# Exponential blocks for VectorE taken also from the next head segment, their products added one part at a time, and a normalisation with three buffers and its broadcast on another queue

## The chip, the cores and the metric

One core of a Trainium2 chip. The metric is device time in microseconds (us) from start to end of one execution. Every kernel was run once with a profile and, except for the first look at the kernel before, three times more, always next to runs of the kernel before on the same chip.

Names: PE is TensorE (matrix products, written to the banks of the memory PSUM), ACT is ScalarE (the exponentials), DVE is VectorE, POOL is GpSimd and SP is SyncE; the last two issue transfers (DMA) here. The engines run side by side, each through its own list of instructions.

## The reference, cut to what matters

Two transformer layers on 2048 tokens of width 512: attention with 32 heads of size 16, then a dense layer of width 1792 with ReLU, each behind a layer norm and with a residual.

```python
qkv = (x @ wqkv).reshape(B, S, 3, H, Dh).transpose(2, 0, 3, 1, 4)     # H = 32, Dh = 16
scores = jnp.einsum("bhqd,bhkd->bhqk", q, k) * (Dh ** -0.5)
p = softmax(scores, axis=-1)
o = jnp.einsum("bhqk,bhkd->bhqd", p, v)
...
x = x + A(layernorm(x)); x = x + B(layernorm(x))                      # this pair twice
```

What costs the time is the softmax's exponential: 2 layers x 32 heads x 2048 x 2048 scores.

## The kernel before

The scores are made in blocks of 128 keys x 512 queries, 4,096 of them. Three blocks make a **slot**: nine (or three, or more) score matmuls write three PSUM banks, one exponential on ScalarE turns them into bf16, and some slots later three product matmuls add them to `ps_o`. A **segment** is the work of four heads for one chunk of 512 queries: 16 key blocks x 4 heads = 64 blocks, 21 slots and a third. A head has only 16 dimensions, so a score matmul uses 32 of the 128 rows of the array, and `g`, the head's place in the group of four, says which 32.

In some slots ScalarE gets only two of the three blocks. VectorE makes the third exponential with integer and polynomial steps; it does so for two slots together, a **pair**. All instructions are put in order by a planner in the kernel's own Python, which keeps estimated clocks (`now_pe`, `now_dve`, `exp_end`) and decides from them. Other matrix products (projections, dense layer) are *owed* in pieces and fitted in between; when five or more are owed, a piece may go ahead past its time limit. That is the *hurry* of the change and of x11; *pace* is how many pieces a slot must take.

The planner's lists of VectorE's work, and a pair's chain of five steps and its six product matmuls:

```python
            if not can:
                for t in dve_q:
                    ready = at(t["deps"], "dve")
                    if ready is not None:
                        can.append((2, ready, t))          # pair chains and everything else alike
...
        steps = (
            (690, lambda: bits(dm, 0x007FFFFF, 0x3E800000)),
            (1260, lambda: step(dy, dm, C2, dm)),
            (1260, lambda: step(dy, dy, C1, dm)),
            (1260, lambda: step(de, dy, C0, di)),
            (690, lambda: bits(di, 0x7F800000, KAPPA_BITS)),
        )
        for n, (cost, fn) in enumerate(steps):
            k = key + (n,) if n + 1 < len(steps) else key
            task(cost, fn, [k], [key + (n - 1,)] if n else [], place=sum("chain" in t for t in dve_q))

    def emit_pair():
        p = pairs.popleft()
        pe_run("v", 3, at([p["key"]], "pe"))
        halves = list(enumerate(p["blocks"]))
        tops = p["di"][:].bitcast(BF16)
        for rhs in (de, de, None):
            for half, (kb, g) in halves:
                pv(p["sg"], kb, g, tops[:, half, 1::2] if rhs is None else rhs[:, half, :])
```

The end of a segment (normalisation): the sums are copied out of `ps_o`, four rows of them go to `c`, VectorE takes the reciprocal, and they come back and are broadcast to `r`, which multiplies `u`:

```python
        if n > 1:
            run_until(("m", n - 2))                         # two buffers
        u, r, c = ubuf[n % 2], rbuf[n % 2], cbuf[n % 2]
...
        def copy():
            nc.vector.tensor_copy(out=u[:], in_=ps_o[:])    # or tensor_add with stored sums
            mark(("po",))
            if not last:
                nc.sync.dma_start(out=c[:], in_=sums)       # 8 KB
                mark(("c", n), lag=2600.0)
...
        def recip():
            nc.vector.reciprocal(out=c[:], in_=c[:])
            nc.sync.dma_start(out=sums, in_=c[:])
            nc.sync.dma_start(out=r[:], in_=...)            # 256 KB, each row of sums to 32 partitions
            mark(("r", n), lag=8500.0)
```

The slot, with the choice of pairs after the scores:

```python
        spare = int(max(need_by - pe_start("s", s_ready), 0.0) / MM)
        short = FLOOR * 1330.0 - level - busy[0] - MM * (1 + (len(pend) > 1))
        times = 1 + min(spare, max(0, math.ceil(short / MM)))    # repeats keep PE busy
        for _ in range(times):
            for w, (sg, kb, g) in enumerate(now):
                nc.tensor.matmul(b[:, w, :], kt[32 * g : 32 * g + 32, kc : kc + P], ...,
                                 tile_position=(32 * g, 0))
        half = None
        if len(now) == W and now[0][0] is sg and not sg["busy"]:
            r = (kb * 4 + g - 2) // W
            if pair_at is not None:
                half = 1 if r == pair_at + 2 else None
            elif len(pairs) < 2 and ...:
                if (
                    ends < now_pe[0] + (21 - r) * 1280.0 + LATE      # in time for this segment's end
                    and now_dve[0] + waiting < now_pe[0] + BACKLOG
                ):
                    half = 0
```

A pair must be complete before its segment's sums can be copied, so no pair is begun near a segment's end.

The softmax here doesn't subtract the row's maximum and nothing guards it: scores larger than these inputs give would overflow.

## Time and profile before

| | before |
|---|---|
| device time, median | 1831.78 us (1831.12 to 1832.17) |
| profiled run, span | 1828.2 us |
| ScalarE busy | 1751.7 us, 96% |
| VectorE busy | 1172.0 us, 64% |
| exponentials of 1536 / 1024 / 512 columns | 1,129 / 236 / 1 |
| first exponential begins, last ends | 17.0 us, 1777.5 us |

A bound of this kind is best read by a budget: the time the exponentials would take if each followed the last at its usual step, and what is lost beside it. The first part of the page holds the busy shares and the chain of work that ended last. The second part shows, in 40 equal slices of the span, VectorE's busy tenths and the granted clock of PE:

```profile
DVE  7436767777676876778442323586678668667673
...
PEclk9999999999999999999999996999999999999998
```

VectorE has room nearly everywhere, and the clock has a dent in the 25th slice. The windows (columns: length, then busy time with number of instructions for PE, PE's weight loads, VectorE, ScalarE, GpSimd, then granted clock, DMA share, GB/s) give the first layer, the stretch of the dent, and the 3.4 us before the clock fell:

```profile
102.00:850.00 748.00, 700.24 (x5803) 220.54 (x5869) 539.94 (x777) 747.02 (x594) 31.47 (x42) 1.00 0.09 19
1085.00:1152.00 67.00, 59.21 (x436) 14.74 (x437) 25.41 (x38) 52.87 (x40) 0.00 (x0) 0.72 0.13 26
1109.60:1113.00 3.40, 0.72 (x10) 0.32 (x12) 2.62 (x5) 0.86 (x1) 0.00 (x0) 1.00 0.05 7
```

In the second row ScalarE works 52.87 of 67 us; elsewhere it hardly rests.

### The profile page before, as it was taken

What the parts mean: (1) busy time and instruction counts of PE and PEld (TensorE: products, weight loads), DVE (VectorE), ACT (ScalarE), POOL (GpSimd) and SP (SyncE); (2) the same over time, 40 slices, a digit from 0 to 9 for tenths busy, and PEclk for the clock granted to TensorE, in tenths of its full rate; (3) what the DMA queues carried; (4) which work ended last, traced back from release to release, by engine and by line L of the source; (5) the groups of instructions that cost most, each with busy time, mean ns of one, the idle gap of its engine ahead of it and who ended that gap; (6) DMA issues with size and microseconds to landing.
All of it is one profiled execution on the core that took longest, in us unless ns stands there. A gap on an engine that the chain in (4) does not pass through costs nothing.

```text
span 1828.2 us, 31187 instructions
## 1 busy us (share of the span) xinstructions
PE 1684.4 (92%) x13531; PEld 533.0 (29%) x13706; DVE 1172.0 (64%) x1795; ACT 1751.7 (96%) x1388; POOL 86.4 (5%) x147
## 2 busy tenths in 40 slices
PE   8899999999999999999999888999999999999987
PEld 3223332222232222322222332232222322232223
DVE  7436767777676876778442323586678668667673
ACT  7999999999999999999999997999999999999981
POOL 1000000100001000010010000001000110001001
PEclk9999999999999999999999996999999999999998
DMA  4000000110001000010000001001000110001101
GB/s 144 1 13 8 19 14 10 39 25 12 8 19 47 8 13 10 23 41 13 13 24 18 1 16 29 13 16 43 16 21 11 34 35 14 16 13 36 28 22 41
DMA packets 38989, 42.37 MB, mean 23 GB/s; under 512 B 19268, under 2 KB 27204, under 8 KB 38852
## 3 DMA queue, kind: packets, MB, share of 16 engines
q1 hardware_dynamic: 32132, 24.37, 5.9%
q0 software_dynamic: 5376, 14.69, 2.9%
q8 instruction: 107, 1.75, 0.4%
q10 hardware_dynamic: 1344, 1.31, 0.2%
q14 instruction: 30, 0.25, 0.0%
HBM read 20.71 MB, written 2.10 MB: 12 GB/s over the span
## 4 chain that ended last, share of the span: by engine, by line
ACT 82%; PE 11%; DVE 4%; DMA 2%; issue 1%; DVEq 0%; SPq 0%
ACT e L957 82%; PE ps_s L934 4%; PE ps_o L722 3%; PE ps_f L378 3%; PE ps_s L1012 1%; DMA c<-u 1%; DVE dy L793 1%; DVE di L763 1%; DVE de L793 0%; DMA r<-u 0%; DVE dm L787 0%; DVE vaug L516 0%; DVE stats L397 0%; PE ps_f L1012 0%; DVE ktp L488 0%
## 5 line engine op out<-in xcount | busy, mean ns | idle before, releaser
L957 ACT ACTIVATE e<-ps_s 128x1536 bf16<-128x1536 f32 (+1 forms) x1366 | 1738.8, 1517 | 22.1 <-PE ps_s L934 21.3
L934 PE MATMUL ps_s<-q,ktp 32*128 32x512 bf16 x7284 | 777.1, 384 | 99.7 <-ACT e L957 77.8
L722 PE MATMUL ps_o<-e,vaug 128*32 128x512 bf16 x3860 | 546.8, 393 | 6.0 <-DVE u L668 4.5
L934 PEld LDWEIGHTS <-ktp 32*128 32x128 bf16 x7284 | 232.2, 92 | 531.3 <-issue 460.3
L722 PEld LDWEIGHTS <-vaug 128*32 128x32 bf16 x4568 | 162.7, 93 | 493.6 <-issue 467.2
L763 DVE TENSOR_SCALAR di<-ps_s 128x512 int32<-128x512 f32 x236 | 162.1, 688 | 91.9 <-PE ps_s L934 89.4
L556 POOL DMA_DIRECT2D w<-in_B_w_dram x112 | 84.0, 750 | 1729.1 <-PE ps_f L378 1594.1
L793 DVE SCALAR_TENSOR_TENSOR de<-dy,di 128x1024 bf16<-128x1024 f32 x118 | 144.3, 1223 | 9.4 <-PE ps_o L722 2.4
L793 DVE SCALAR_TENSOR_TENSOR dy<-dm 128x1024 f32<-128x1024 f32 x118 | 144.1, 1221 | 2.5
L793 DVE SCALAR_TENSOR_TENSOR dy<-dy,dm 128x1024 f32<-128x1024 f32 x118 | 144.0, 1221 | 2.1
L566 DVE TENSOR_SCALAR ht<-ps_f 128x512 bf16<-128x512 f32 x98 | 67.5, 689 | 107.2 <-PE ps_f L378 101.6
L378 PE MATMUL ps_f<-xn2T,w 128*128 128x512 bf16 x346 | 114.3, 384 | 5.9 <-issue 1.9
L378 PE MATMUL ps_f<-w,ht 128*128 128x512 bf16 x349 | 110.6, 384 | 4.1 <-issue 3.0
L681 DVE SCALAR_TENSOR_TENSOR ot<-u,mask,r 128x512 bf16<-128x512 f32 (+1 forms) x67 | 46.5, 694 | 71.1 <-DMA r<-u 70.9
L787 DVE TENSOR_SCALAR di<-di 128x1024 int32<-128x1024 int32 x118 | 82.0, 695 | 3.2
L525 DVE TENSOR_SCALAR q<-ps_f,qmask 128x512 bf16<-128x512 f32 x78 | 55.7, 745 | 42.9 <-PE ps_f L378 41.0
L722 PE MATMUL ps_o<-de,vaug 128*32 128x512 bf16 x472 | 82.9, 382 | 0.0
L787 DVE TENSOR_SCALAR dm<-di 128x1024 int32<-128x1024 int32 x118 | 81.5, 691 | 1.5
L378 PE MATMUL ps_f<-xnT,wqkv 128*128 128x512 bf16 x235 | 77.5, 386 | 4.6 <-issue 2.1
L378 PE MATMUL ps_f<-wo,ot 128*128 128x512 bf16 x195 | 63.9, 384 | 2.9 <-issue 2.2
L722 PE MATMUL ps_o<-di,vaug 128*32 128x512 bf16 x236 | 57.7, 391 | 0.0
L670 DVE COPY u<-ps_o 128x512 f32<-128x512 f32 x48 | 33.1, 690 | 29.5 <-PE ps_o L722 29.3
(89 smaller groups left out, 536.2 us busy)
## 6 DMA issues: line engine op xcount, KB each, us to landing
r<-u SPq DMA_DIRECT2D x63, 256.0 KB
w<-in_B_w_dram POOLq DMA_DIRECT2D x112, 128.0 KB, 2.6
out_dram<-x SPq DMA_DIRECT2D x16, 128.0 KB
x<-in_A_x_dram SPq DMA_DIRECT2D x14, 128.0 KB
w<-in_B_w_dram SPq DMA_DIRECT2D x1, 1792.0 KB
wqkv<-in_A_wqkv_dram ACTq DMA_DIRECT2D x2, 512.0 KB
c<-u SPq DMA_DIRECT2D x63, 8.0 KB
u<-c SPq DMA_DIRECT2D x63, 8.0 KB
```

What stands on the lines that cost most here:

```text
L378: nc.tensor.matmul(b, lhsT, rhs, start=(i == 0), stop=(i == n - 1))
L525: return nc.vector.tensor_scalar(out=qbuf[n % 2][e][:], in0=b, scalar1=qmask[e][:, 0:1], scalar2=None, op0=ALU.mult)
L556: nc.gpsimd.dma_start(out=w1buf[n % NW1][:], in_=B_w1[:, ft * P : (ft + 1) * P].rearrange("(c p) f -> p c f", p=P),)
L566: nc.vector.tensor_scalar(out=ht[ft], in0=b, scalar1=0.0, scalar2=None, op0=ALU.max)
L670: nc.vector.tensor_copy(out=u[:], in_=ps_o[:])
L681: nc.vector.scalar_tensor_tensor(out=ot[t][:, a : a + w], in0=u[:, a : a + w], scalar=mask[e][:, 0:1], in1=r[:, a : a + w], op0=ALU.mult, ...
L722: nc.tensor.matmul(ps_o[32 * g : 32 * g + 32, :], vaug[sg["l"]][kb][:, 4 * sg["T"] + g, 2 * e : 2 * e + 32], rhs, start=g not in sg["begun ...
L763: first = nc.vector.tensor_scalar(out=di[:, half, :].bitcast(I32), in0=src, scalar1=EXP_BIAS, scalar2=0.0, op0=ALU.add, op1=ALU.max,)
L787: nc.vector.tensor_scalar(out=out[:].bitcast(I32), in0=di[:].bitcast(I32), scalar1=keep, scalar2=put, op0=ALU.bitwise_and, op1=ALU.bitwise_or,
L793: nc.vector.scalar_tensor_tensor(out=out[:], in0=x[:], scalar=c, in1=y[:], op0=ALU.add, op1=ALU.mult)
L934: nc.tensor.matmul(b[:, w, :], kt[32 * g : 32 * g + 32, kc : kc + P], qbuf[sg["n"] % 2][sg["e"]][32 * g : 32 * g + 32, :], start=True, sto ...
L957: ex = nc.scalar.activation(out=eb[:, :m, :], in_=b[:, :m, :], func=ACTF.Exp, scale=1.0 / (LOG2E * UNIT),)
```

## The change

The intent: more of the exponentials on VectorE, since ScalarE is the bound. Where a pair of the present segment would come too late, its two blocks may come from the next segment, whose end is far off. For that to be affordable, the pair chains get the lowest priority on VectorE; the pair's products are added a part (two matmuls) at a time where PE has room; the normalisation gets three buffers and its large broadcast another queue. Cut to its core:

```diff
+    NU = 3
...
+    HURRY = 2.0
...
-    acc = [x[:, k, :] for x in [dm, dy] + dis for k in range(2)]
+    acc = [... for x in kt01 + kt2] + [... for x in va2]     # layer 1's stored sums: in dead K and V tiles of layer 0
...
-    de = sb([P, 2, QS], BF16, "de")
+    des = [sb([P, 2, QS], BF16, f"de{n}") for n in range(2)]
...
-            limit_now = limit if owed[0] < 5.0 else now_pe[0] + 1000.0
+            limit_now = limit if owed[0] < 5.0 or not hurry[0] else now_pe[0] + 1000.0
...
-                        can.append((2, ready, t))
+                        can.append((3 if "chain" in t else 2, ready, t))
...
-        if n > 1:
-            run_until(("m", n - 2))
-        u, r, c = ubuf[n % 2], rbuf[n % 2], cbuf[n % 2]
+        if n >= NU:
+            run_until(("m", n - NU))
+        u, r, c = ubuf[n % NU], rbuf[n % NU], cbuf[n % NU]
...
-            nc.sync.dma_start(
+            nc.gpsimd.dma_start(
                 out=r[:],
...
-            task(cost, fn, [k], [key + (n - 1,)] if n else [], place=sum("chain" in t for t in dve_q))
+            task(cost, fn, [k], [key + (n - 1,)] if n else [])
...
-    def emit_pair():
-        p = pairs.popleft()
-        pe_run("v", 3, at([p["key"]], "pe"))
+    def emit_pair(limit):
+        p = pairs[0]
+        ready = at([p["key"]], "pe")
+        while p["parts"] and pe_start("v", ready) + MM <= limit:
+            rhs = p["parts"].pop(0)
+            pe_run("v", 1, ready)
+            for half, (kb, g) in enumerate(p["blocks"]):
+                pv(p["sg"], kb, g, rhs(half))
...
+            later = next((x for x in itertools.islice(blocks, 70) if x[0] is not mine), None)
+            if pair_at == no:
+                half, take = 1, pairs[-1]["sg"]
+            elif len(pairs) < 2 and ...:
+                if now_dve[0] + waiting < now_pe[0] + BACKLOG:
+                    if not mine["busy"] and ends < now_pe[0] + left_here * 430.0 - 1300.0:
+                        half, take = 0, mine
+                    elif (
+                        left_here < 40 and later and not later[0]["busy"]
+                        and later[0]["l"] == mine["l"] and not pairs_for(later[0])
+                        and at([("q", later[0]["n"])], "pe") is not None
+                    ):
+                        half, take = 0, later[0]
+            if half is not None:
+                pair_at = no + 2 if half == 0 else None
+                if take is not mine:
+                    blocks.appendleft(now.pop())
+                    now.append(later)
+                    blocks.remove(later)
...
-            emit_pair()
+            emit_pair(max(exp_end[no - 1] + ACT_TO_PE, exp_end[no] - MM - PE_TO_ACT - SWITCH - 100.0))
```

## The prediction

> **What bounds the kernel now.** I read the busy line and the chain of work that ended last, then the groups kept apart by shape, then ScalarE's waits, then the timeline where it waits.
>
> ```profile
> PE 1684.4 (92%) x13531; PEld 533.0 (29%) x13706; DVE 1172.0 (64%) x1795; ACT 1751.7 (96%) x1388; POOL 86.4 (5%) x147
> ...
> ACT 82%; PE 11%; DVE 4%; DMA 2%; issue 1%; DVEq 0%; SPq 0%
> ```
>
> ScalarE (ACT) is busy 96% and makes 82% of the chain: 1,366 exponentials, one per "slot" of three 128x512 score blocks. PE's 92% is no bound: 7,284 score matmuls are issued for 4,096 score blocks, the other 3,188 are repeats that keep it busy.
>
> ```profile
> L957 ACT ACTIVATE e<-ps_s 128x1536 bf16<-128x1536 f32 x1129 | 1557.4, 1594 | 19.9 <-PE ps_s L934 19.1
> L957 ACT ACTIVATE e<-ps_s 128x1024 bf16<-128x1024 f32 x236 | 259.7, 1150 | 2.3 <-PE ps_s L934 2.2
> L763 DVE TENSOR_SCALAR di<-ps_s 128x512 int32<-128x512 f32 x236 | 162.1, 688 | 91.9 <-PE ps_s L934 89.4
> L793 DVE SCALAR_TENSOR_TENSOR de<-dy,di 128x1024 bf16<-128x1024 f32 x118 | 144.3, 1223 | 9.4 <-PE ps_o L722 2.4
> L787 DVE TENSOR_SCALAR di<-di 128x1024 int32<-128x1024 int32 x118 | 82.0, 695 | 3.2
> ```
>
> In 236 slots VectorE takes the third block (118 pairs), so ScalarE does 1024 columns instead of 1536. Successive instructions overlap, so their means cannot be subtracted. I took start-to-start times from the trace: median 1.331 us after a 1536-column exponential, 0.904 us after a 1024-column one. **A block moved to VectorE saves 0.427 us.**
>
> With these steps the ideal run of the exponentials is 1129 x 1.331 + 236 x 0.904 + 0.5 = 1716.5 us. The trace's run is from 16.99 to 1777.5 = 1760.5 us, so 44 us are lost between. By place: about 7.5 us in the first 102 us, 17.4 us between 1093 and 1152 us, and 19 us thinly spread over all the rest. Before the first and after the last exponential stand 17.0 and 50.7 us. The median device time, 1831.8, is 3.6 us over the profiled span, 1828.2.
>
> The 17.4 us are one event. First the chain in order of time, then the SP queue's issues, the timeline of PE and ACT, and the windows:
>
> ```profile
> 1085.78 0.70 DVE u L668
> 1086.47 0.02 issue
> 1086.49 5.01 DMA c<-u
> ...
> 1103.16 6.30 DMA c<-u
> ```
>
> ```profile
> 1102.58 0.53 SPq L691 DMA_DIRECT2D r<-u  x1
> 1103.16 0.52 SPq L673 DMA_DIRECT2D c<-u  x1
> ```
>
> ```profile
> 1112.28 0.40 PE L722 MATMUL ps_o<-e,vaug 128*32 128x512 bf16 x4 [3.62 <-DVE u L668]
> ...
> 1113.76 1.45 ACT L957 ACTIVATE e<-ps_s 128x1536 bf16<-128x1536 f32 x1 [3.30 <-PE ps_s L934]
> ...
> 1115.71 1.45 ACT L957 ACTIVATE e<-ps_s 128x1536 bf16<-128x1536 f32 x1 [0.49 <-PE ps_s L934]
> ```
>
> ```profile
> 1114.00:1130.00 16.00, 15.53 (x97) 3.18 (x95) 2.95 (x6) 11.97 (x9) 0.00 (x0) 0.50 0.15 30
> 1130.00:1150.00 20.00, 19.53 (x109) 3.65 (x109) 13.28 (x16) 13.65 (x11) 0.00 (x0) 0.50 0.07 15
> ```
>
> This is the second half of layer 1's first chunk, where a head segment has only 16 blocks and lasts 16/3 x 1.331 = 7.1 us. Each ends in a normalisation: sums to c, reciprocal, back to u, broadcast to r. The 8 KB transfer c<-u is issued behind the 256 KB r<-u of the segment before, on the same SP queue, and takes 5 to 6.3 us. So these loops run at 9.0 us (1094.19, 1103.16, 1112.25), slower than segments arrive. With two u/r/c buffers the lag ends in a wait: ps_o isn't emptied, PE stands 3.62 us, its granted clock falls to 0.50 for some 36 us (seventh number of the last two rows), and every exponential there waits 0.5 us for scores.
>
> **What the Trainium skill says.** "ScalarE: Activation LUTs", What ACT_TABLE_LOAD costs: 0.833 ns a column; the trace agrees, 0.427 us for 512 columns. "VectorE: DVE Perf Modes", the perf-mode tier table: fp32 scalar operations on SBUF run at twice the rate of two-input ones; the trace agrees, 695 against 1223 ns. "TensorE: Matmul & The Clock Gate", Part 1: a window of about 3.4 us of idleness halves PE's clock. The trace agrees on the fall (3.62 us idle, clock 0.50), but shows a return only after about 36 us, not after one busy window. "DMA: Bandwidth & Descriptors", SWDGE vs HWDGE vs iDMA: the engines take turns between the queues of the two kinds, and SWDGE descriptors need an SBUF path that VectorE can lock. The trace has no r<-u on the GpSimd queue, so neither is shown yet.
>
> **The change part by part.**
>
> *More pairs.* The built programs, read in order: 1,129 / 236 / 1 exponentials of 1536 / 1024 / 512 columns become 1,067 / 298 / 1. That is 149 pairs instead of 118, of which 53 take their blocks from the next segment. 62 blocks x 0.427 = **26.5 us off ScalarE**. None are added in the first chunk of layer 1: its first half stays excluded because it stores sums, its second because its runs are short.
>
> *Cost on VectorE.* A pair is 2 x 0.688 + 2 x 0.693 + 3 x 1.222 = 6.43 us; 31 x 6.43 = 199 us. From 102 to 850 us it is busy 540 of 748 us; 16 pairs more, in 14 us less, make 643 of 734, 88%. The second layer's stretch gives the same. It fits, as the added priority lets other tasks pass the chains, but there is less slack. The first step now ends a median 0.57 us after its slot's exponential begins (99th percentile 1.2), ahead of when its bank is wanted.
>
> *PE.* 124 more product matmuls net, 588 fewer score matmuls: no bound. But a borrowed block comes with its own row group of the array, and in 84 of the 106 borrowed slots it is the row group of one of the two others, so these matmuls cannot overlap; the planner doesn't count that. 15 of the 84 issue the scores three times, 23 twice, 46 once. By an estimate from the 216 ns the kernel's plan gives a pass, and about 0.87 us between a bank's release and the need for its scores, that costs 0.45 us in 15 slots, 0.1 in 23 and 0.05 in 46: **+11 us at worst, I take 7**.
>
> *One part at a time, and no hurry below a pace of 2.* Six product matmuls at once delay scores; in the trace the slots around them lose 4.9 us in all, and single delays of 0.3 us elsewhere some 3 us. I take **-5 us**. More 1024-column slots, each losing 0.044 us on average, **+3**, and a fuller VectorE **+3**. So the thin losses go from 19 to 27.
>
> *Three buffers, r on the GpSimd queue.* c no longer stands behind r. A segment's normalisation has 3 x 7.1 = 21 us against an estimated 13 to 14 us (kernel's lags 3.0 and 9.5 us plus VectorE), so PE should not stop and its clock should not fall: **17.4 becomes about 2, -15.4 us**.
>
> *The start* is the same instruction for instruction for the first 300 score matmuls, so its loss of about 7 us stays.
>
> *The tail.* Before, the last-but-one normalisation gets its reciprocal only at 1771.9, behind pair chains, and VectorE waits 2.07 us for r<-u before the last normalisation, which begins at 1781.4. In the new order the reciprocal comes one and a half chains before the end: **about -2.5 us**.
>
> Sum: 17.0 + (1067 x 1.331 + 298 x 0.904 + 0.5 = 1690.1) + 7 + 2 + 27 + 48.2 + 3.6 = 1794.9. Against 1831.8 that is 36.9 us less, 2.0%. I have been cautious with the 7 us for row groups, and the wait constants have plainly been fitted to measurements, so I go a little below: **1792 us**.
>
> **The rivals.**
> (a) *The spared time comes back as waits of ScalarE for scores*: a VectorE at 88%, in fixed order, empties banks and sums late, or row groups collide more dearly. For: the 89.4 us it now waits for scores before its first steps is most of its slack. Against: its steps run at or below the planned durations (1.22 us against 1.26). With 0.1 us lost in each of 298 slots and all row-group costs: about 1810.
> (b) *The new r<-u is slow*: GpSimd is locked out by the VectorE steps of the fast mode (298 of 0.69 us), or stands in its queue behind a weight load waiting for PE; then a VectorE that waits for r in order stops everything. Against: the weight loads on that queue land in a median 2.6 us. For: untested here. If the stall at 1093 to 1152 stays whole: about 1808.
> (c) *It was only the stall*: if nearly all thin loss goes too, 1780.
>
> **Range and chances.** The exponentials' 26.5 us are nearly sure, the stall's 15 likely. What remains open is the thin loss, 15 to 40 us, and that alone moves the time by 25. 8 in 10: 1780 to 1806. The 2% line lies at 1795.1, hardly above my sum: faster 0.57, same 0.42, slower 0.01.
>
> **What would show it.** Right: 1,067 and 298 exponentials with steps of 1.331 and 0.904 us; no wait of ScalarE over 1 us after 110 us; no stretch of granted clock near 0.5 in the middle; c<-u landing in about 2 to 3 us; VectorE near 1,370 us busy. The row-group step is wrong if slots with a borrowed block lose no more than other 1024-column slots. The prediction falls if the clock still drops near the layer's first chunk, or if ScalarE's summed waits for scores exceed some 40 us.

## The result, and the profile after

| | before | after |
|---|---|---|
| device time, median of 4 runs | 1831.65 us (1831.12 to 1832.17) | 1798.97 us (1797.80 to 1800.75) |
| ratio | | 0.9822 (95% interval 0.9805 to 0.9839) |
| profiled run, span | 1828.2 us | 1795.7 us |

The ratio is the mean time of one kernel's runs over that of the other's of the same rounds, so not quite the ratio of the medians; so it is for every ratio below. At a threshold of 2%: "same", 1.8% less.

The busy line, the 40 slices and the chain on the page of the kernel after:

```profile
PE 1657.4 (92%) x13064; PEld 515.0 (29%) x13242; DVE 1356.0 (76%) x2012; ACT 1729.2 (96%) x1388; POOL 133.8 (7%) x210
...
DVE  7438688889989898888642315999888898898863
...
PEclk9999999999999999999999999999999999999999
...
ACT 77%; PE 19%; DVE 2%; issue 1%; DMA 1%; DVEq 0%; ACTq 0%
...
r<-u POOLq DMA_DIRECT2D x63, 256.0 KB, 7.1
```

The dent in the clock is gone and VectorE is fuller by 184 us. But PE's share of the chain has gone *up*, from 11% to 19%: ScalarE waits for PE in more places, each of them short. The last line is the broadcast on its new queue, 7.1 us from issue to landing: in 45 of the 46 times when no other transfer shared the queue, the trace has at most four of its packets under way at once. The groups by shape confirm the new numbers of exponentials:

```profile
L1009 ACT ACTIVATE e<-ps_s 128x1536 bf16<-128x1536 f32 x1067 | 1485.5, 1562 | 9.1 <-PE ps_s L1002 7.8
L1009 ACT ACTIVATE e<-ps_s 128x1024 bf16<-128x1024 f32 x298 | 324.4, 1089 | 6.3 <-PE ps_s L1002 5.2
```

And the windows, first the same 748 us, then the stretch in which the kernel before stood still:

```profile
102.00:850.00 748.00, 699.86 (x5604) 211.22 (x5672) 634.32 (x891) 743.29 (x600) 54.20 (x72) 1.00 0.09 20
1075.00:1130.00 55.00, 49.29 (x461) 16.50 (x464) 32.69 (x48) 54.52 (x43) 4.79 (x7) 1.00 0.20 36
```

ScalarE now works 54.52 of 55 us there. In the first layer VectorE is at 634 of 748 us, 85%.

The full budget, from the start times of the 1,366 exponentials in both traces. A slot's loss is its start-to-start time over the usual step, the most frequent one (1.331 us after 1536 columns, 0.904 us after 1024; both traces give these; the median after 1024 columns, which holds waits too, is 0.912 before and 0.905 after). Slots 672 to 865 are the first chunk of layer 1 and what follows it, where the stall was:

| us | before | after | predicted |
|---|---|---|---|
| until the first exponential | 17.0 | 16.9 | 17.0 |
| exponentials at their steps | 1716.5 | 1690.1 | 1690.1 |
| lost in slots 1 to 75 | 7.9 | 6.6 | 7 |
| lost in slots 75 to 672 | 10.5 | 17.4 | |
| lost in slots 672 to 865 | 19.0 | 3.1 | |
| lost after slot 865 | 6.3 | 13.8 | |
| (the last three together) | 35.8 | 34.3 | 29 |
| after the last exponential | 50.7 | 47.6 | 48.2 |

So of the 32.5 us by which the span shrank, 26.4 are the exponentials handed over and 3.1 the tail. The stall's end gave about 16 more, and nearly all of it went back into slots that start a little late. This is where the expected gain went, and the experiments ask why.

The chain in order of time shows how such a loss looks. First the kernel after, around a segment's end:

```profile
140.29 0.98 PE ps_o L748 x9
...
142.15 1.47 PE ps_s L1002 x9
143.62 0.02 issue
143.64 17.21 ACT e L1009 x14
160.85 0.04 issue
160.89 0.82 PE ps_s L1002 x9
...
169.53 1.41 PE ps_s L1002 x9
170.95 0.02 issue
170.97 2.37 ACT e L1009 x2
```

Nine score matmuls are three passes over three blocks. At 160.89 they take 0.82 us, at 142.15 and 169.53 1.4 to 1.5 us. The slow ones belong to slots in which a borrowed block has the same `g`, the same 32 rows of the array, as another block of the slot: 87 slots of the built program. The Trainium skill, "TensorE: Matmul & The Clock Gate", Part 3 (The mechanism), says that a weight load overlaps running matmuls only when its row group differs; this trace agrees, with 0.6 us more for nine matmuls. By the start times these 87 slots lose 14.9 us: 47 with one pass 0.074 each, 24 with two passes 0.187, 16 with three passes 0.433. (The expectation of x1 counted 13.9 us.)

The tail, in VectorE's timeline, before and after:

```profile
1771.91 0.24 DVE L689 RECIPROCAL c<-c 128x16 f32<-128x16 f32 x1
...
1780.74 0.75 DVE L681 SCALAR_TENSOR_TENSOR ot<-u,mask,r 128x512 bf16<-128x512 f32 x1 [2.07 <-DMA r<-u]
...
1781.41 0.72 DVE L702 STREAM_SHUFFLE r<-u 128x512 f32<-128x512 f32 x1
```

```profile
1728.09 0.24 DVE L715 RECIPROCAL c<-c 128x16 f32<-128x16 f32 x1
...
1748.62 0.69 DVE L695 COPY u<-ps_o 128x512 f32<-128x512 f32 x1 [7.93 <-PE ps_o L748]
...
1749.36 0.72 DVE L728 STREAM_SHUFFLE r<-u 128x512 f32<-128x512 f32 x1
```

Before, the last normalisation (the shuffle) began 3.9 us after the last exponential's end (1777.5), behind a wait for the normalisation ahead of it. After, it begins 1.2 us behind that end (1748.2), with nothing of the earlier normalisation in its way: that one's reciprocal came 20.1 us ahead of the last exponential's end, and not 5.6.

### The profile page after: what moved, and what is told of

Its sections match the earlier page's. It is cut to its first block, busy times and chain, and to the rows that moved or that the text cites. A ratio compares the mean times of both kernels' runs of the same rounds, so it can differ in the third digit from the quotient of the medians.

```text
span 1795.7 us, 30592 instructions
## 1 busy us (share of the span) xinstructions
PE 1657.4 (92%) x13064; PEld 515.0 (29%) x13242; DVE 1356.0 (76%) x2012; ACT 1729.2 (96%) x1388; POOL 133.8 (7%) x210
## 4 chain that ended last, share of the span: by engine, by line
ACT 77%; PE 19%; DVE 2%; issue 1%; DMA 1%; DVEq 0%; ACTq 0%
ACT e L1009 77%; PE ps_s L1002 7%; PE ps_o L748 5%; PE ps_f L397 4%; PE ps_s L1065 1%; DMA wqkv<-in_A_wqkv_dram 1%; DVE di L794 1%; PE ps_f L1065 0%; DVE vaug L535 0%; DVE u L695 0%; DVE stats L416 0%; DVE ktp L507 0%; DVE q L544 0%; PE ps_o L1065 0%; DMA x<-in_A_x_dram 0%
## 5 line engine op out<-in xcount | busy, mean ns | idle before, releaser
L1009 ACT ACTIVATE e<-ps_s 128x1536 bf16<-128x1536 f32 (+1 forms) x1366 | 1716.3, 1459 | 15.3 <-PE ps_s L1002 13.0
L1002 PE MATMUL ps_s<-q,ktp 32*128 32x512 bf16 x6696 | 753.5, 379 | 83.7 <-ACT e L1009 63.4
L794 DVE TENSOR_SCALAR di<-ps_s 128x512 int32<-128x512 f32 x298 | 204.8, 687 | 106.3 <-PE ps_s L1002 104.0
L825 DVE SCALAR_TENSOR_TENSOR dy<-dm 128x1024 f32<-128x1024 f32 x149 | 182.1, 1222 | 4.4
L825 DVE SCALAR_TENSOR_TENSOR dy<-dy,dm 128x1024 f32<-128x1024 f32 x149 | 181.5, 1218 | 3.3
L825 DVE SCALAR_TENSOR_TENSOR de<-dy,di 128x1024 bf16<-128x1024 f32 x149 | 180.6, 1212 | 1.8
L717 POOL DMA_DIRECT2D r<-u x63 | 45.6, 723 | 1245.2 <-DMA u<-c 472.6
L748 PE MATMUL ps_o<-de,vaug 128*32 128x512 bf16 x596 | 110.1, 382 | 0.0
L819 DVE TENSOR_SCALAR dm<-di 128x1024 int32<-128x1024 int32 x149 | 105.4, 708 | 0.6
L819 DVE TENSOR_SCALAR di<-di 128x1024 int32<-128x1024 int32 x149 | 104.0, 698 | 2.0
L585 DVE TENSOR_SCALAR ht<-ps_f 128x512 bf16<-128x512 f32 x98 | 67.5, 689 | 43.1 <-PE ps_f L397 40.2
L707 DVE SCALAR_TENSOR_TENSOR ot<-u,mask,r 128x512 bf16<-128x512 f32 (+1 forms) x67 | 48.4, 722 | 15.8 <-DMA r<-u 15.4
```

The source lines that it names most:

```text
L585: nc.vector.tensor_scalar(out=ht[ft], in0=b, scalar1=0.0, scalar2=None, op0=ALU.max)
L707: nc.vector.scalar_tensor_tensor(out=ot[t][:, a : a + w], in0=u[:, a : a + w], scalar=mask[e][:, 0:1], in1=r[:, a : a + w], op0=ALU.mult, ...
L717: nc.gpsimd.dma_start(out=r[:], in_=bass.AP(tensor=sums.tensor, offset=sums.offset, ap=[list(sums.ap[0]), [0, 32], [1, QS]],),)
L748: nc.tensor.matmul(ps_o[32 * g : 32 * g + 32, :], vaug[sg["l"]][kb][:, 4 * sg["T"] + g, 2 * e : 2 * e + 32], rhs, start=g not in sg["begun ...
L794: first = nc.vector.tensor_scalar(out=di[:, half, :].bitcast(I32), in0=src, scalar1=EXP_BIAS, scalar2=0.0, op0=ALU.add, op1=ALU.max,)
L819: nc.vector.tensor_scalar(out=out[:].bitcast(I32), in0=di[:].bitcast(I32), scalar1=keep, scalar2=put, op0=ALU.bitwise_and, op1=ALU.bitwise_or,
```

## The experiments

The theory was: the change removes 26.4 us from ScalarE and the stall, and pays part of it back in late slots, above all those with two blocks in one row group. Rivals: the payback comes from VectorE's fullness, from PE bursts of a pair's products, or from the slower hurry rule; the stall's end comes from the third buffer rather than from the queue; and the borrowing isn't the source of the gain at all. Eleven kernels were run, in three groups on three chips (x1 to x4, x5 to x8, x9 to x11), all with a correct result. "Lost" is the sum of all slots' losses in the profiled run; it holds 1 to 4 us more where the clock fell near 90 us, which it did in all but the change's first, x1's and x11's, and about 1 us more where it fell near 1,200 us (x2, x6, x8, x10, x11). At the 2% threshold x2 is "faster", x1, x7 and x9 are "unclear" and all others "same"; differences between the runs are read from the ratios.

| run | ratio to before (95%) | median us | pairs | lost us |
|---|---|---|---|---|
| the change, first run | 0.9822 (0.9805 to 0.9839) | 1798.97 | 149 | 41.1 |
| x5, the change again | 0.9835 (0.9820 to 0.9850) | 1800.52 | 149 | 43.4 |
| x1, no row clash | 0.9786 (0.9771 to 0.9801) | 1791.96 | 149 | 33.4 |
| x2, one pass in a clash | 0.9774 (0.9758 to 0.9790) | 1789.73 | 150 | 40.2 (slowest run) |
| x3, no borrowing | 0.9979 (0.9964 to 0.9994) | 1826.97 | 102 | 30.7 |
| x4, normalisation alone | 0.9958 (0.9943 to 0.9973) | 1822.92 | 120 | 37.1 |
| x6, pair at once | 0.9887 (0.9872 to 0.9902) | 1810.03 | 151 | 55.2 |
| x7, chains not last | 1.0196 (1.0179 to 1.0213) | 1867.21 | 155 | 113.2 |
| x8, two buffers | 0.9862 (0.9847 to 0.9877) | 1806.18 | 149 | 49.2 |
| x9, x1 with one part a slot | 0.9793 (0.9779 to 0.9808) | 1793.40 | 148 | 34.8 |
| x10, r on SP | 0.9920 (0.9904 to 0.9937) | 1816.41 | 149 | 60.7 |
| x11, hurry kept | 0.9852 (0.9838 to 0.9867) | 1804.54 | 149 | 47.0 |

### x1: borrowed blocks that share no row group

```diff
-            later = next((x for x in itertools.islice(blocks, 70) if x[0] is not mine), None)
+            rows_used = {x[2] for x in now[:-1]}
+            first_kb = pairs[-1]["blocks"][0][0] if pair_at == no else -1
+            later = next((x for x in itertools.islice(blocks, 70)
+                if x[0] is not mine and x[2] not in rows_used and x[1] > first_kb), None)
```

> The changed kernel, but a borrowed block is chosen from the next segment so that its row group is none of the other two blocks' of its slot (and the pair's second block comes from another key block); 149 pairs as in the changed kernel, 2 slots with two blocks of one row group instead of 84. My theory: in the changed kernel's trace such slots start their exponential 0.075, 0.18 and 0.42 us late with one, two and three passes of score matmuls, 13.9 us in all, so this runs in 1786 us (1783 to 1789), ratio to the kernel before about 0.975. Rival, the fuller VectorE is what costs: the exponentials come as late as before, 1797 to 1800 us.

Measured: 1791.96 us, ratio 0.9786; faster than both kernels. The plan is the change's, slot for slot in the number of product matmuls, but only 2 slots clash. The chain of this kernel through the stretch shown above:

```profile
139.56 8.56 ACT e L1017 x7
148.12 0.04 issue
148.16 1.04 PE ps_s L1010 x12
...
150.98 22.15 ACT e L1017 x18
```

Where PE's slow passes broke the chain at 142.15 and 169.53, exponentials follow one another. It gained less than the clash slots lost: of the whole loss, 7.7 us went (41.1 to 33.4). Slot by slot, the 87 that clashed in the change lose 2.2 us here instead of 14.9. But the 214 other pair slots lose 6.1 instead of 2.3, and all the rest 1.2 more. So an exponential that came late for one reason had hidden another; presumably PE caught up during its delay, which no run shows. So the clash costs, by what its removal gives, between 0.0036 and 0.0049 of the time before (against the two runs of the change), 7 to 9 us.

### x2: a clash, but one pass of scores only

```diff
         times = 1 + min(spare, max(0, math.ceil(short / MM)))
+        if len({x[2] for x in now}) < len(now):
+            times = 1
```

> The changed kernel, but slots in which two blocks share a row group issue their score matmuls once, never two or three times (91 such slots, 150 pairs). Row-group theory: each of the 91 loses the 0.075 us of a one-pass slot, 7 us instead of 13.9, so about 1791 us. If repeats cost nothing (VectorE theory): 1797 to 1800 us.

Measured: 1789.73 us, ratio 0.9774. There are still 91 clash slots, at 0.037 us each, 3.4 us in all. So it is not the shared row group as such but its repetition for the sake of PE's clock that was dear. The planner repeats the passes into time it counts as spare at 216 ns a pass, and with a clash a pass takes 0.48 us (1.41 to 1.48 for three). x1 and x2 can't be told apart in time (their intervals overlap).

Its profiled run was its slowest, 1795.95 us, 6 to 8 us above its other three, and shows what may be the price of fewer repeats. The windows of the 3.4 us before the clock fell and the next ones, then the change in the same window:

```profile
1116.30:1119.75 3.45, 2.26 (x23) 0.61 (x21) 3.42 (x6) 3.28 (x3) 0.35 (x1) 1.00 0.11 20
1119.75:1123.10 3.35, 3.35 (x23) 0.78 (x23) 3.29 (x4) 2.48 (x2) 0.33 (x1) 0.50 0.20 35
```

```profile
1119.75:1123.10 3.35, 2.72 (x27) 0.88 (x28) 3.19 (x5) 3.35 (x4) 0.68 (x1) 1.00 0.13 20
```

With PE busy 2.26 us of such a window and no idle gap over 1.18 us, the clock fell to 0.50 for 10.2 us; with 2.72 us it stayed. The three runs without a kept trace have a higher mean clock (0.996 to 0.997 against 0.993), so the fall does not come every time; that fewer repeats are its reason is not shown.

### x3: no borrowing

```diff
-                        left_here < 40 and later and not later[0]["busy"]
+                        False and later and not later[0]["busy"]
```

> The changed kernel without borrowing from the next segment: 102 pairs instead of 149, no row-group clash. Theory: 47 pairs less put 47 x 2 x 0.427 = 40 us back on ScalarE, the clash loss of 14 us goes: 1799 + 40 - 14 = 1825 us (1821 to 1829). If ScalarE's exponentials were not the bound, less than half of the 40 us would show: below 1808 us.

Measured: 1826.97 us, ratio 0.9979, as expected. Only 102 pairs are left (the new rule for a segment's own pairs is stricter than the old), so the exponentials at their steps need 1730.2 us, 40 us more than in the change, while 10 us less is lost. But this kernel also has 16 pairs fewer than the kernel before (13.7 us more at the steps), which hides what its other parts gain: the stretch of the stall loses 2.5 us here, as in the change. So the run shows what the 47 pairs are worth, 26 to 28 us in time; it does not show that the other parts gain nothing by themselves.

### x4: the normalisation's part alone, put into the kernel before

```diff
+    NU = 3
...
-        u, r, c = ubuf[n % 2], rbuf[n % 2], cbuf[n % 2]
+        u, r, c = ubuf[n % NU], rbuf[n % NU], cbuf[n % NU]
...
-            nc.sync.dma_start(
+            nc.gpsimd.dma_start(
                 out=r[:],
...
-            mark(("r", n), lag=8500.0)
+            mark(("r", n), lag=9500.0)
```

> The kernel before with only three u/r/c buffers, r<-u on the GpSimd queue and the two planned lags of the change; 120 pairs, none borrowed. Theory: TensorE no longer stands in the first chunk of layer 1 and keeps its clock, so 17.4 us of loss become about 1 and two pairs more give 1.7: about 1814 us (1811 to 1817). Rival, the freed stall comes back elsewhere or the slower r<-u stops VectorE: 1825 us or more.

Measured: 1822.92 us, ratio 0.9958. A miss: 8 us gained, by the ratio, instead of 17. Slots 672 to 865 still lose 9.4 us, and the tail grew by 3.1. The chain there, VectorE's timeline and PE's:

```profile
1110.32 5.22 DMA c<-u
...
1118.20 7.52 DMA r<-u
```

```profile
1125.79 0.75 DVE L682 SCALAR_TENSOR_TENSOR ot<-u,mask,r 128x512 bf16<-128x512 f32 x1 [2.39 <-DMA r<-u]
1126.46 0.68 DVE L669 TENSOR_TENSOR u<-di,ps_o 128x512 f32<-128x512 f32 x1
```

```profile
1127.19 0.40 PE L723 MATMUL ps_o<-e,vaug 128*32 128x512 bf16 x4 [2.37 <-DVE u L669]
```

The first cause is that `c<-u` took 5.22 us, on its own queue: it landed 0.2 us after the `r<-u` that GpSimd had issued 2.0 us before it. That made the next `r<-u` late. VectorE works in order: the multiplication that waits for `r` stands ahead of the copy that would empty `ps_o`, PE waits for that copy, and the clock fell again, for 13.7 us. In the change's trace one `c<-u` is as late (5.2 us, issued at 1099.79):

```profile
1105.04 0.25 DVE L715 RECIPROCAL c<-c 128x16 f32<-128x16 f32 x1 [5.28 <-DMA c<-u]
```

But there the corresponding multiplication, at 1114.95, comes behind the copy, at 1113.62, and its one long wait for `r` in this stretch (3.4 us, at 1090.85) is over before PE has finished the sums. So the stall's end in the change is not a matter of buffers and queue alone; the new order on VectorE belongs to it, by these timelines; no run changes the order there and nothing else.

### x5: the change again, as a control for x6 to x8

> The changed kernel itself, as control on the chip of these runs: 1798 to 1801 us, ratio about 0.982, as when it was first measured. If the row-group saving of x1 (7 us against the first measurement, 14 expected) was partly a difference of chips, this one comes out near 1805 us.

Measured: 1800.52 us, ratio 0.9835. Slots 75 and later lose the same as in the first run (17.4, 3.1 and 13.8 us); the start lost 2.3 us more, because the clock fell at 90.7 us. That is a difference between runs and not of the kernel, and it is the size of the scatter between the change's own runs.

### x6: a pair's six products at once

```diff
-            emit_pair(max(exp_end[no - 1] + ACT_TO_PE, exp_end[no] - MM - PE_TO_ACT - SWITCH - 100.0))
+            emit_pair(1e18)
```

> The changed kernel, but a finished pair's six product matmuls are put on TensorE's queue at once, as in the kernel before (151 pairs, 75 slots of clashing row groups). My prediction's step: parts instead of bursts save up to 5 us, so this one loses 3 to 5 us less 1.7 us for two pairs more: about 1801 us. Rival, the form of emission does not matter because the last parts are flushed at once anyway: 1796 to 1798 us.

Measured: 1810.03 us, ratio 0.9887: 10 us slower than the change on the same chip, twice what was expected at most. Pair slots without a clash lose 18.8 us (2.3 in the change). The chain in the stretch shown before:

```profile
139.83 1.35 ACT e L1009
141.18 0.04 issue
141.22 0.82 PE ps_s L1002 x9
142.05 0.98 PE ps_o L748 x9
...
150.07 1.04 PE ps_s L1002 x12
151.12 0.98 PE ps_o L748 x9
```

The nine product matmuls in one piece (three of a slot and six of a pair) are 0.98 us in which no scores are made. The change has such pieces too (the first line of its chain above, at 140.29), but only where the planner sees room: all six products of a pair stand before one slot's scores 98 times there and 151 times here, and these slots lose 5.8 us there and 20.3 here. So, by this comparison, it is the burst without room that costs.

### x7: pair chains with the same priority as everything else

```diff
-                        can.append((3 if "chain" in t else 2, ready, t))
+                        can.append((2, ready, t))
...
-            task(cost, fn, [k], [key + (n - 1,)] if n else [])
+            task(cost, fn, [k], [key + (n - 1,)] if n else [], place=sum("chain" in t for t in dve_q))
```

> The changed kernel, but VectorE's pair chains keep their old place, ahead of other tasks that are not yet begun (155 pairs). Theory: the late reciprocal brings the tail back from 47.6 to 50 us or more, and the layer's first chunk waits again for reciprocals, as the run with the normalisation parts alone did (loss 9 us there against 3): with 5 us won by six more pairs, about 1802 us (1798 to 1808). Rival, priority does nothing for the time: 1794 us by the six pairs.

Measured: 1867.21 us, ratio 1.0196, slower than the kernel before and 65 us above what was expected, a clear miss. 155 pairs fit, but 113.2 us are lost, 35.1 of them at once. The waits of ScalarE (sum, times, longest), in the change and here:

```profile
ACT e L1009 <- PE ps_s L1002: 13.0, 40, 3.0
```

```profile
ACT e L1009 <- PE ps_s L1002: 74.0, 104, 34.8
```

The stop comes where the second layer's first segment needs all of the first layer: the last chunk's projection, dense layer and layer norm run at 907 to 942 us with nothing beside them. That the chains had pushed them back is read from the edit, which changes the priority alone and with it the plan. So the low priority is what makes a VectorE at 85% bearable.

### x8: two buffers, broadcast on GpSimd

```diff
-    NU = 3
+    NU = 2
```

> The changed kernel with two u/r/c buffers instead of three, r<-u still on the GpSimd queue. Theory, it is the third buffer that lets a normalisation of 13 us outlast a segment of 7.1: the stall with the falling clock returns, 8 to 16 us, 1807 to 1815 us. Rival, the queue alone is enough because c<-u lands in 1.5 us: 1798 to 1801 us.

Measured: 1806.18 us, ratio 0.9862. Slots 672 to 865 lose 8.7 us against 3.1, and the clock fell there for 6.8 us. The third buffer is worth 5.6 us by this stretch, 5.7 by the medians on one chip; the intervals of the ratios just overlap.

### x9: x1 with at most one part of a pair in a slot

```diff
-        while p["parts"] and pe_start("v", ready) + MM <= limit:
+        while p["parts"] and most > 0 and pe_start("v", ready) + MM <= limit:
+            most -= 1
```

In x1 98 slots still add all three parts at once, and the slots after them lose 6.4 us. The theory was that spreading them would get those back.

> The version without row-group clashes (x1), and at most one part of a pair, two product matmuls, in a slot (148 pairs; slots that get all three parts fall from 98 to 2). In x1's trace the exponentials after slots with more than one part came 11 us late in all. If these bursts are what took back half of x1's saving, about 1785 us (1783 to 1788), ratio 0.974. Rival, the thin losses just move to other slots: 1790 to 1793 us as x1.

Measured: 1793.40 us, ratio 0.9793, a miss: no gain over x1. Slots with all three parts fell from 98 to 2, and 34.8 us are lost instead of 33.4; the loss moved to the slots with one or two parts. So the remaining thin loss does not hang on bursts of this size; it went along with the parts to where they were put. Which of PE's waits makes it, the runs do not settle.

### x10: three buffers, broadcast back on SP

```diff
-            nc.gpsimd.dma_start(
+            nc.sync.dma_start(
                 out=r[:],
```

> The changed kernel with three u/r/c buffers, but r<-u back on the SP queue. The loops of c behind r ran at 9.0 us against 7.1 us per segment; over the chunk's eight segments that lags by up to 15 us, of which a third buffer can take 7. Theory: some of the stall returns, 3 to 8 us, 1803 to 1808 us. Rival, three buffers are enough alone: 1798 to 1801 us.

Measured: 1816.41 us, ratio 0.9920, worse than expected. Slots 672 to 865 lose 19.0 us, as in the kernel before. VectorE's timeline, and a window:

```profile
1103.39 0.25 DVE L715 RECIPROCAL c<-c 128x16 f32<-128x16 f32 x1 [7.56 <-DMA c<-u]
...
1112.38 0.25 DVE L715 RECIPROCAL c<-c 128x16 f32<-128x16 f32 x1 [6.25 <-DMA c<-u]
```

```profile
1110.00:1120.00 10.00, 10.00 (x47) 2.24 (x44) 4.11 (x7) 5.31 (x5) 0.00 (x0) 0.50 0.16 33
```

`c` stands behind `r` again, the clock falls (for 34 us), and ScalarE works 5.31 of 10 us. In the change's order the new queue is worth 16 us (19.0 against 3.1), more than the third buffer (5.6, x8); and three buffers on the old queue lose as much in this stretch as the kernel before did with two.

### x11: the hurry kept at every pace

```diff
-    HURRY = 2.0
+    HURRY = 0.0
```

> The changed kernel, but with the old rule that weight-matmul pieces that are owed go ahead past the limit whatever the pace (149 pairs). My prediction put some 3 us on the new rule: 1802 to 1804 us. Rival, it changes nothing measurable: 1798 to 1801 us.

Measured: 1804.54 us, ratio 0.9852, as expected. Against the change's 0.9822 and 0.9835 this is 3 to 5.5 us slower (0.0017 and 0.0030 of the time before); the interval overlaps with that of the control, so only the direction, hardly the size, is shown.

## Why the prediction was right or wrong

The range held the result, and "within 2%" came, to which I had given 0.42 against 0.57 for faster. The point was 7 us too low. By its own steps:

**More pairs: right.** 1,067 and 298 exponentials at unchanged steps of 1.331 and 0.904 us, 26.4 us less. I called 0.904 us the median; in the trace before it is the most frequent step, and the median is 0.912. What a moved block saves without waits is 0.427 us all the same.

**VectorE: right.** 1,356 us busy against some 1,370, and in the first layer 634 of 748 us, 85%, against 643 of 734, 88%. I wrote that it fits because other tasks may pass the chains; x7 shows how much hangs on that, 67 us.

**The stall: right, with two corrections.** It is gone: 3.1 us are lost in its stretch, of which about 1.4 us is in its place. First, the 8 KB `c<-u` landed 1.8 to 1.9 us after its issue in 58 of 63 cases, sooner than the 2 to 3 us I named; before, when issued 0.6 to 1.9 us behind `r<-u`, in 5.0 to 6.3. But my "c no longer stands behind r" holds only in part: of the six issued in the change while an `r<-u` was under way, two took 3.7 and 5.2 us and landed 0.2 us after it, though on another queue (one took 2.35, three 1.8). The 1.5 us in the expectation of x8 is too small. x10 against the change confirms the queue as worth 16 us. Second, x4 shows that buffers and queue without the new order give only half.

**The tail: right.** 47.6 against 48.2.

**Row groups: the mis-sized term.** I worked out 0.45, 0.1 and 0.05 us for slots with three, two and one pass, "+11 us at worst", and took 7. Measured: 0.433, 0.187 and 0.074, in sum 14.9 us in 87 slots (the 84 I named and three that are no pair slots). The dear case was right; the two common cases were set too low, probably because I took all the 0.87 us between a bank's release and the need for its scores as free, and product matmuls share that time; no run tests this. What is more, such delays are not additive: x1 took 12.6 us of them away and gained 7 to 9.

**One part at a time, more short slots, a fuller VectorE: the other half of the miss.** I netted these to +1 us. In the change's trace slots without a clash do lose about as much as before (19.4 us after the 75th), which looks like a confirmation. x1 corrects that: with the clashes gone, slots after the 75th lose 26.5 us, against 35.8 before less 17.4 for the stall, 18.4. So the net was about +8, and 7 of it had been hidden behind the clashes. The part "-5" was even too small: x6 shows 10 us for it in the denser schedule. So what I missed is on the side of the plus, presumably in slots that are slower because more is done in them. x9 rules out bursts of three parts as the reason; which wait it is stays open.

**The discount.** My sum was 1794.9. The thin losses made it 5.3 us more, start, tail and the difference to the device time 1.3 us less: 1799. From the sum I then went down by 2.9 us because the constants of the waits seemed fitted to measurements. No line of the profile supported that; it is 2.9 of the 7 us, and with it the point came to lie clearly on the wrong side of the 2% line.

**Rivals.** (a) was the right kind and half the size: late slots, but 0.05 us for each of the 298 pair slots and not 0.1. (b) did not happen: `r<-u` landed in 7.0 to 7.7 us in all 63 cases beside 298 fast-mode steps on VectorE, and VectorE's waits for it fell from 70.9 to 15.4 us. The lock can have cost little: the five issues that took longest on GpSimd, 0.83 to 1.22 us against a median of 0.71, all ran beside such a step, but 17 others beside one took 0.75 us at most. (c) is refuted: 34 us were still lost.

## What to carry to other kernels

When work is taken off the bounding engine, add up the start times of its instructions against their usual step: the time comes back in delays of a tenth of a microsecond of which the list of waits shows a part (13.0 of 41.1 us in the change), and since one delay hides another, only an experiment tells what removing one is worth. A scheduler that moves a block from one place to another should check every resource that the block carries with it, here its row group of the array; a rule of two lines (x2: one pass in such slots; x1: another block) was worth 7 to 9 us of a change that gained 33. A small transfer that many wait for should not stand on the queue of a large one; here another queue freed most but not all of them.

## What the Trainium skill lacked or had wrong

- "TensorE: Matmul & The Clock Gate", Part 1 (What's actually happening): it gives one idle window of about 3.4 us as the reason of a fall, and one busy window for the return. Here the clock fell after windows of 3.4 us that were far from idle: PE busy 2.26 us with no gap over 1.18 us (x2), and 1.95 us with no gap over 0.52 us (before, at 92.4 us), as well as after 0.72 us (before, at 1113.0). It stayed with 2.64 us (x1) and 2.72 us (the change). So a low busy share is enough, without an idle window. No sharp limit comes out: with 2.23 us it stayed too (before, 1106.2 to 1109.6 us). (The page's section on a second failure mode knows falls by short idle times, but no share.) The return came after one window at 92.4 us, but after 11 (37.5 us) at 1113.0 and after 10 in x10, though PE was busy all the time in the window shown there. Why it took so long was not tested.
- The same page, Part 3 (Packing small matmuls): it has the rule that only different row groups overlap, but no cost for breaking it. Here nine 32-row matmuls of 512 columns took 1.41 to 1.48 us with two of three blocks in one row group, and 0.82 us with none.
- "DMA: Bandwidth & Descriptors" has no figure for a small transfer beside a large one: 8 KB took 1.8 us alone, 5.0 to 6.3 us when issued 0.6 to 1.9 us behind 256 KB on one queue, and 1.8 to 5.2 us when the 256 KB were on another queue.
- "ScalarE: Activation LUTs", What ACT_TABLE_LOAD costs: 186 ns and 0.833 ns a column, with an overlap of 93 ns, would give by an estimate steps of 1.373 us for 1536 columns and 0.946 us for 1024; the usual steps measured were 1.331 and 0.904.
